# Routed rows turned by 64x64 products with an identity, eight tiles at a time, in rounds one and two of a convolution with routed experts

## The chip, the cores and the metric

The kernel runs on one core of a Trainium2 chip. The metric is the time of one execution on the device in microseconds (us); less is better. The change is judged by the median of several executions of each kernel.

## What is computed

The input `x` is 8 sequences of 5056 tokens with 128 channels; `h` is one filter of the same length for each channel. The first half is a causal convolution by way of a long Fourier transform, the second sends each of the 40,448 results to one of 16 experts, chosen in two steps.

```python
Xf = np.fft.rfft(x, n=L, axis=1); Hf = np.fft.rfft(h, n=L, axis=0)      # L = 2 * 5056
y = np.fft.irfft(Xf * Hf[None], n=L, axis=1)[:, :S]                     # then rows: x = y.reshape(N, 128)
g_idx = np.argmax(x @ w_group, axis=1)                                  # 4 groups, weight g_w by softmax
for g in range(4):
    xg = x[g_idx == g]; e_idx = np.argmax(xg @ w_expert[g], axis=1)     # 4 experts each, weight e_w by softmax
    for e in range(4):
        xe = xg[e_idx == e]
        out[rows of xe] = (g_w * e_w)[:, None] * (np.maximum(xe @ w1[g, e], 0) @ w2[g, e])
```

## The kernel before, in words

**Three rounds.** `ROUNDS` splits the filter and the 8 sequences into three rounds of three: the filter with sequences 0 and 1, then 2 to 4, then 5 to 7. For each round r, `stage1(r)` does the first part of the forward transform (lines 441 and 447, alternating: two of three steps by quadruples of 64x64 products, the third by 128x128 products), `groups(r)` does the rest of it, the multiplication by the filter and the first part of the inverse, pair of frequencies by pair (`forward` line 548, `multiply` line 568 on VectorE, `inverse` line 615, copied out of PSUM by ScalarE in line 631), and `side(r)` does the last part of the inverse and the routing. All of line 548's and line 615's products are 64x64 too, four of them in the four quarters of the array. Results between the parts go through HBM (`zd`, `zr`).

**The side work.** `side(r)` goes through 8 octaves of 8 of the 64 residues. For each octave it makes two lumps (`mm` line 756, `rest` line 771) that accumulate in the two PSUM banks `py0` and `py1`, and ScalarE copies them to `yT` (line 779): 128 channels on the partitions, T x 128 tokens along the row, T = 10 tiles in round one (r = 0) and 15 in the others. From `yT` come two things:

- the logits: `lm` multiplies `yT` by the routing weights in four column strips of 32 (line 829), ScalarE copies them to `lT` (line 835); `lt` turns `lT` by transposes (line 840), ScalarE copies them to `lg` (line 844), and `gate_math`, a row of small VectorE operations, finds expert, weight and place of each token;
- the rows to be sent: `rows(i)` turns four tiles of 128 tokens at a time by four 128x128 transposes into one bank (line 815), and one ScalarE copy (line 819) puts them into a tile `rw` in 16-bit halves. GpSimd then scatters each tile's 128 rows to the experts' lists in HBM (`scatter`, line 895).

`bank()` (line 798) hands out `py0` and `py1` in turn to `lm`, `lt` and `rows`; the lumps use the same two banks. Whoever writes a bank waits until ScalarE has copied what was there.

**What sets the order.** The program is written out in the order in which `weave` calls its pieces: a main list (stage 1 and groups, then the experts' matmuls) and beside each stretch of it one round's side work, whose pieces have due times (`at`, in eighths of a round). An engine executes its instructions in that order. The side work of round one lies beside round two's stage 1 and groups, that of round two beside round three's, that of round three beside the first experts' matmuls. Since the main list advances in steps of a stage 1 step, a forward pair or an inverse pair, two pieces with near due times can fall into the same gap and then stand directly one behind the other. The scatters are paced by a count of matmul time that the program keeps itself (`worked`, `clock`), not by a clock of the chip.

Names in the rows below: `pp` is a two-bank PSUM tile of stage 1 and groups, `cg` and `ns` the constants of a pair and their negative (made by ScalarE, line 526), `hg` the filter's spectrum, `zm` and `zt` what the lumps read back, `px`, `pz`, `ptr` PSUM tiles of the experts.

Of the kernel before, what the change touches and what calls it, by code (L numbers as in the profile page):

```python
# [13 lines left out]
U16 = mybir.dt.uint16  # L14
# [6 lines left out]
B, S, D = 8, 5056, 128  # L21
# [11 lines left out]
ROW = D + 2  # L33
# [10 lines left out]
COL, COLR = 4 / 2400, 1 / 2400 + 25e-6  # L44
NW_MAX = (NTOK + NE * 127) // BLK
T0, H0 = 1000, 2000
GP = 128
# [31 lines left out]
RH = 8  # L79
# [142 lines left out]
def columns(nu):  # L222

    n = 8 * nu * NH
    t = (n + GP - 1) // GP
    return t, n - (t - 1) * GP
# [11 lines left out]
class Kernel:  # L238
# [481 lines left out]
    def side(self, r):  # L720
        nc, cx = self.nc, self.cx
# [59 lines left out]
        def lump(k):  # L781
            def f():
                if k == 0 and r < 2:
                    nc.vector.memset(self.smask, 1.0)
                    first = self.smask[:, 0:NE * T].rearrange("p (e t) -> p e t", t=T)[:, :, 0:1]
                    nc.vector.memset(first, 0.0)
                for n in range(4 * k, 4 * k + 4):
                    mm(n)
                    if n % QB == QB - 1:
                        load(n // QB + 2)  # L790
                rest(4 * k)

            return f

        T, last = columns(nu)
        od = {}

        def bank():
            od["bank"] = 1 - od.get("bank", 1)
            return self.ps.tile([128, 512], F32, name=f"py{od['bank']}", bufs=1)  # L800

        def rows(i):

            if i == 0:
                od["rw"] = []
                od["o"] = od.get("o", -1) + 1
            if i % 2 == 0:
                while self.sends and self.sends[0][0] <= (8 * r + od["o"] - 2, i // 2):
                    self.send()
                od["rw"].append(cx.tile([128, RH, 2 * ROW], U16, name="rw", bufs=4))  # L810
            n = min(4, T - 4 * i)
            pt = bank()
            for j in range(n):
                k = (4 * i + j) * GP
                last = nc.tensor.transpose(  # L815
                    out=pt[:, j * D:(j + 1) * D], in_=self.yT[:, k:k + GP], identity=self.ident
                )
            self.worked(last, n * D * COL / 2)
            nc.scalar.copy(  # L819
                out=od["rw"][i // 2][:, 4 * i % RH:4 * i % RH + n, 0:2 * D].rearrange("p j (h d) -> p j h d", h=2),  # L820
                in_=pt[:, 0:n * D].bitcast(U16).rearrange("p (j d h) -> p j h d", d=D, h=2),
            )

        nsl = (T + 3) // 4

        def lm():
# [23 lines left out]
        def advance(g):  # L850
            return lambda: next(g, None)

        def both(*fs):
            return lambda: [f() for f in fs]

        at = []
        more = [lambda i=i: rows(i) for i in range(2, nsl)]
        for o in range(N2 // 8):
            math = {}
            ops = self.gate_math(od, math, b0 * S + o * 8, T, nu, REST if r < 2 else REST2)  # L860
            sends = [self.scatter(math, k, GP if k < T - 1 else last, r, T) for k in range(T)]
            if r < 2:
                t = 8 * o
                at.append((t, lump(2 * o), False))
                at.append((t + 3, lump(2 * o + 1), False))
                at.append((t + 4.7, both(lm, lambda: rows(0)), False))
                at.append((t + 6.4, both(lt, lambda: rows(1)), False))
                at.append((t + 9.5, both(*more), False))
                at += [(t + 6.5 + 5.6 * k / (NMATH + REST), advance(ops), True) for k in range(NMATH + REST)]
                at.append((t + 12.15, lambda o=o, s=sends: self.sends.extend(((8 * r + o, i // RH), f, self.clock + READY + SPREAD * i) for i, f in enumerate(s)), True))  # L870
            else:

                t = 6 * o
                at.append((t, lump(2 * o), False))
                at.append((t + 2, lump(2 * o + 1), False))
                at.append((t + 3, both(lm, lambda: rows(0)), False))
                at.append((t + 4, both(lt, lambda: rows(1)), False))
                at.append((t + 5, both(*more), False))
                at += [(t + 4.02 + 3.3 * k / (NMATH + REST2), advance(ops), True) for k in range(NMATH + REST2)]
                at.append((t + 7.4, lambda o=o, s=sends: self.sends.extend(((8 * r + o, i // RH), f, self.clock + READY + SPREAD * i) for i, f in enumerate(s)), True))  # L880
# [971 lines left out]
```

## Time and profile before

| what | value |
|---|---|
| runs | 1656.35, 1651.05, 1656.14 us, median 1656.14 |
| the profiled execution | 1647.12 us, span 1645.4 us |
| TensorE (PE) busy | 1586.1 us, 96% of the span |
| VectorE (DVE), ScalarE (ACT), GpSimd (POOL) busy | 80%, 66%, 46% |
| mean granted TensorE clock | 0.992 of full speed |
| side work of rounds one and two | from about 150 to 587 us of the span |
| line 815, all rounds | 320 transposes, 49.7 us busy |

A row of the timeline has the start in us from the span's start, the time from the first start to the last modelled end of the instructions merged in it, the engine (PE for matmuls, PEld for weight loads), the line, the operation, output and inputs by the program's names, shapes, and a count. A matmul's modelled end lies well after the moment at which the next one can start, so TensorE's pace is read from start to start, not from the second column. A matmul in float32 that isn't a transpose has two records in the trace, a transpose has one: "x32" of line 441 are 16 products.

### The profile page before, as it was taken

What the parts mean: (1) busy time and instruction counts of PE and PEld (TensorE: products, weight loads), DVE (VectorE), ACT (ScalarE), POOL (GpSimd) and SP (SyncE); (2) the same over time, 40 slices, a digit from 0 to 9 for tenths busy, and PEclk for the clock granted to TensorE, in tenths of its full rate; (3) what the DMA queues carried; (4) which work ended last, traced back from release to release, by engine and by line L of the source; (5) the groups of instructions that cost most, each with busy time, mean ns of one, the idle gap of its engine ahead of it and who ended that gap; (6) DMA issues with size and microseconds to landing.
All of it is one profiled execution on the core that took longest, in us unless ns stands there. A gap on an engine that the chain in (4) does not pass through costs nothing. (4 is left out here: it accounts for less than half of the span.)

```text
span 1645.4 us, 46854 instructions
## 1 busy us (share of the span) xinstructions
PE 1586.1 (96%) x16576; PEld 1241.5 (75%) x16576; DVE 1313.1 (80%) x2911; ACT 1092.4 (66%) x2161; POOL 760.0 (46%) x730
## 2 busy tenths in 40 slices
PE   8998999989999989999999999999999999999997
PEld 8776755557766547877777778788888888888997
DVE  6654699885688887788877788888888888887898
ACT  5564555545555556777777777677777777777875
POOL 1462144342465545155555556445555554334555
PEclk9999999999999989999999999999999999999999
DMA  7798688877789977766666655558866687555666
GB/s 209 237 294 240 185 259 268 277 226 223 216 273 302 289 209 190 191 172 177 181 169 179 176 142 151 146 139 235 196 155 171 163 233 181 138 137 151 172 171 166
DMA packets 400429, 328.58 MB, mean 200 GB/s; under 512 B 165740, under 2 KB 343921, under 8 KB 400168
## 3 DMA queue, kind: packets, MB, share of 16 engines
q1 hardware_dynamic: 371304, 269.43, 59.9%
q0 software_dynamic: 20608, 41.79, 7.5%
q10 hardware_dynamic: 8256, 14.10, 3.0%
q8 instruction: 137, 2.24, 0.6%
q14 instruction: 124, 1.02, 0.2%
HBM read 207.21 MB, written 96.08 MB: 184 GB/s over the span
## 5 line engine op out<-in xcount | busy, mean ns | idle before, releaser
L895 POOL DMA_INDIRECT srt<-rw,pos x320 | 336.6, 1052 | 390.7 <-PE py L815 61.7
L1512 POOL DMA_INDIRECT out<-orow,ids x188 | 195.8, 1041 | 222.5 <-PE px L1437 52.9
L1512 POOL DMA_INDIRECT out<-orow,sids x92 | 97.2, 1057 | 113.3 <-PE px L1441 46.3
L568 DVE TENSOR_TENSOR y<-pp,hg 128x768 f32<-128x768 f32 (+1 forms) x108 | 92.3, 855 | 60.2 <-ACT hg L558 31.6
L615 PE MATMUL pp<-y,cg 64*64 64x384 f32 (+1 forms) x1504 | 117.5, 443 | 6.6 <-DVE m L568 4.3
L548 PE MATMUL pp<-st,cg 64*64 64x192 f32 (+1 forms) x1588 | 117.4, 407 | 0.7 <-PE pp L615 0.4
L462 DVE TENSOR_TENSOR st<-pp,odd 128x320 f32<-128x320 f32 x96 | 46.9, 488 | 74.4 <-ACT odd L461 74.2
L631 ACT COPY zs<-pp 128x768 f32<-128x768 f32 (+1 forms) x106 | 75.7, 714 | 45.0 <-PE pp L615 35.3
L1446 DVE SCALAR_TENSOR_TENSOR h0l<-px,h0h 128x512 fp32r<-128x512 f32 (+1 forms) x109 | 73.3, 673 | 34.5 <-ACT h0h L1445 33.7
L1446 DVE SCALAR_TENSOR_TENSOR h2l<-px,h2h 128x512 fp32r<-128x512 f32 (+1 forms) x112 | 75.3, 672 | 29.7 <-ACT h2h L1445 27.8
L1445 ACT ACTIVATE h0h<-px 128x512 fp32r<-128x512 f32 (+1 forms) x109 | 63.9, 587 | 52.0 <-PE px L1441 48.0
L779 ACT COPY yT<-py 128x474 f32<-128x474 f32 (+1 forms) x96 | 44.2, 513 | 78.0 <-PE py L771 72.6
L1446 DVE SCALAR_TENSOR_TENSOR h3l<-px,h3h 128x512 fp32r<-128x512 f32 (+1 forms) x111 | 74.5, 671 | 26.1 <-ACT h3h L1445 25.2
L756 PEld LDWEIGHTS py<-ig,zm 126*64 126x64 f32 x2048 | 74.1, 137 | 26.8 <-ACT rw L819 9.8
L756 PE MATMUL py<-ig,zm 126*64 126x79 f32 x2048 | 82.8, 235 | 11.6 <-ACT rw L819 6.9
L548 PEld LDWEIGHTS pp<-st,cg 64*64 64x64 f32 x1588 | 60.8, 134 | 42.7 <-issue 35.4
L615 PEld LDWEIGHTS pp<-y,cg 64*64 64x64 f32 x1504 | 56.7, 133 | 47.0 <-issue 31.8
L568 DVE TENSOR_TENSOR m<-pp,hg 128x768 f32<-128x768 f32 (+1 forms) x108 | 91.5, 847 | 0.0
L599 POOL TENSOR_TENSOR y<-y,m 128x512 f32<-128x512 f32 x40 | 51.0, 1277 | 73.6 <-DVE m L589 40.9
L1445 ACT ACTIVATE h3h<-px 128x512 fp32r<-128x512 f32 (+1 forms) x111 | 65.3, 588 | 28.2 <-PE px L1441 27.3
L819 ACT COPY rw<-py 128x1024 uint16<-128x1024 uint16 (+1 forms) x88 | 80.8, 937 | 1.7 <-PE py L815 0.5
L1445 ACT ACTIVATE h1h<-px 128x512 fp32r<-128x512 f32 (+1 forms) x111 | 65.2, 587 | 21.7 <-PE px L1441 19.5
(479 smaller groups left out, 5087.7 us busy)
## 6 DMA issues: line engine op xcount, KB each, us to landing
wr<-in_moe_w SPq DMA_DIRECT2D x373, 256.0 KB
zm<-zd SPq DMA_DIRECT2D x64, 378.0 KB
cg<-in_c_g SPq DMA_DIRECT2D x106, 224.0 KB
zd<-zs SPq DMA_DIRECT2D x50, 384.0 KB
hg<-hd SPq DMA_DIRECT2D x68, 128.0 KB
xt<-in_x ACTq DMA_DIRECT2D x52, 160.0 KB
zm<-zd SPq DMA_DIRECT2D x32, 252.0 KB
zd<-zs SPq DMA_DIRECT2D x31, 256.0 KB
```

What stands on the lines that cost most here:

```text
L462: nc.vector.tensor_tensor(out=all_st[:, 0:2 * HALF, d], in0=even, in1=odd, op=ALU.add)
L548: last = nc.tensor.matmul(px[c * 64:c * 64 + 64, b, to], lhsT=k, rhs=data[:, of], start=begin, stop=i == len(steps) - 1 or p == 0 and i == ...
L568: nc.vector.tensor_tensor(out=t[:, :, 0:w].rearrange("p t (r u d) -> p t r u d", r=2, u=nu), in0=taken(px, part).unsqueeze(1).broadcast_to ...
L599: (nc.gpsimd if r == 0 else nc.vector).tensor_tensor(out=y[:, :, 0:w], in0=y[:, :, 0:w], in1=m[:, :, 0:w], op=ALU.add)
L615: last = nc.tensor.matmul(pz[c][h:h + 64, 0:w], lhsT=wt[c * 64:c * 64 + 64, k + h:k + h + 64], rhs=y[c * 64:c * 64 + 64, part, 0:w], start ...
L631: nc.scalar.copy(out=z[:, 0:n, 0:w], in_=pp[:, 0:n, 0:w])
L756: last = nc.tensor.matmul(pys[q][c:c + 64, col(n, u)], lhsT=zms[q][:, n % QB, k:k + 64], rhs=self.ig[:, 0:NH], start=n % QB == 0 and u == ...
L819: nc.scalar.copy(out=od["rw"][i // 2][:, 4 * i % RH:4 * i % RH + n, 0:2 * D].rearrange("p j (h d) -> p j h d", h=2), in_=pt[:, 0:n * D].bi ...
L895: ins = self.nc.gpsimd.indirect_dma_start(out=self.srt, out_offset=bass.IndirectOffsetOnAxis(ap=k["pos"][0:p, j:j + 1], axis=0), in_=k["rw ...
L1445: nc.scalar.activation(out=hh, in_=p, func=AF.Relu)
L1446: nc.vector.scalar_tensor_tensor(out=hl, in0=p, scalar=0.0, in1=hh.bitcast(F32), op0=ALU.max, op1=ALU.subtract)
L1512: ins = self.nc.gpsimd.indirect_dma_start(out=self.a["out"], out_offset=bass.IndirectOffsetOnAxis(ap=ids, axis=0), in_=o, in_offset=None, ...
```

## The change

In rounds one and two (r < 2) `rows` is no longer called. A new function `eight` turns up to eight tiles at a time, each by four plain products of a 64x64 block of `yT` with a 64x64 identity, in the four quarters of the array; the two halves of the channels go to two banks, and each bank is copied by one ScalarE copy for all eight tiles. `eight(0)` has a due time of its own, 5.6, between those of `lm` (4.7) and `lt` (6.4), which now stand alone; `eight(1)`, the remaining 2 tiles in round one and 7 in round two, takes the place of the last calls of `rows` at 9.5. Round three (r = 2) is as before.

```diff
--- before.py
+++ after.py
@@ -821,6 +821,32 @@
                 in_=pt[:, 0:n * D].bitcast(U16).rearrange("p (j d h) -> p j h d", d=D, h=2),
             )
 
+        def eight(i):
+
+            if i == 0:
+                od["rw"] = []
+                od["o"] = od.get("o", -1) + 1
+            while self.sends and self.sends[0][0] <= (8 * r + od["o"] - 2, i):
+                self.send()
+            t = cx.tile([128, RH, 2 * ROW], U16, name="rw", bufs=4)
+            od["rw"].append(t)
+            n = min(8, T - 8 * i)
+            pts = [bank(), bank()]
+            for j in range(n):
+                k = (8 * i + j) * GP
+                for b in (0, 64):
+                    for c in (0, 64):
+                        last = nc.tensor.matmul(
+                            pts[b // 64][c:c + 64, j * 64:j * 64 + 64], lhsT=self.yT[b:b + 64, k + c:k + c + 64],
+                            rhs=self.ident[b:b + 64, b:b + 64], start=True, stop=True, tile_position=(b, c),
+                        )
+            self.worked(last, n * D * COL / 2)
+            for b in range(2):
+                nc.scalar.copy(
+                    out=t[:, 0:n, 0:2 * D].rearrange("p j (h d) -> p j h d", h=2)[:, :, :, b * 64:b * 64 + 64],
+                    in_=pts[b][:, 0:n * 64].bitcast(U16).rearrange("p (j d h) -> p j h d", d=64, h=2),
+                )
+
         nsl = (T + 3) // 4
 
         def lm():
@@ -863,9 +889,10 @@
                 t = 8 * o
                 at.append((t, lump(2 * o), False))
                 at.append((t + 3, lump(2 * o + 1), False))
-                at.append((t + 4.7, both(lm, lambda: rows(0)), False))
-                at.append((t + 6.4, both(lt, lambda: rows(1)), False))
-                at.append((t + 9.5, both(*more), False))
+                at.append((t + 4.7, lm, False))
+                at.append((t + 5.6, lambda: eight(0), False))
+                at.append((t + 6.4, lt, False))
+                at.append((t + 9.5, lambda: eight(1), False))
                 at += [(t + 6.5 + 5.6 * k / (NMATH + REST), advance(ops), True) for k in range(NMATH + REST)]
                 at.append((t + 12.15, lambda o=o, s=sends: self.sends.extend(((8 * r + o, i // RH), f, self.clock + READY + SPREAD * i) for i, f in enumerate(s)), True))
             else:
```

In these two rounds 200 transposes become 800 products (8 octaves of 10 and of 15 tiles), and the 56 copies of line 819 become 64. The orders of VectorE, GpSimd and SyncE have the same instructions in the same places. Three places of TensorE's order follow; names with `py0` and `py1` are the two banks, `pp`, `cg`, `ns` and `y` belong to the groups, and what stands in brackets is what an instruction waits for.

TensorE before, round one's third octave: `lm`, `rows(0)`, a forward pair, `lt`, `rows(1)`.

```order
L829 MATMUL py0_3867<-yT_333,wge_113 32x384 [waits PE_49]
L829 MATMUL py0_3867<-yT_333,wge_113 32x384 x3
L815 MATMUL py1_3875<-ident_132,yT_333 128x128 [waits PE_49]
L815 MATMUL py1_3875<-ident_132,yT_333 128x128 x3
L548 MATMUL pp_3885<-st_94,cg_3436 64x384 x4
```

The same place in the changed kernel (line 855 is the old 829).

```order
L855 MATMUL py0_3931<-yT_333,wge_113 32x384 [waits PE_49]
L855 MATMUL py0_3931<-yT_333,wge_113 32x384 x3
L839 MATMUL py1_3939<-ident_132,yT_333 64x64 [waits PE_49]
L839 MATMUL py1_3939<-ident_132,yT_333 64x64
L839 MATMUL py0_3940<-ident_132,yT_333 64x64 [waits Activation_49]
L839 MATMUL py0_3940<-ident_132,yT_333 64x64
```

Here `eight(0)` stands directly behind `lm`, and its third product writes `py0`, into which `lm` has just written; the transposes before wrote the other bank.

TensorE before, round one's fifth octave: the end of a forward pair, `lt`, `rows(1)`, an inverse.

```order
L548 MATMUL pp_4802<-st_94,ns_4741 64x192 x3
L840 MATMUL py0_4828<-ident_132,lT_4764 128x128 [waits Activation_49]
L840 MATMUL py0_4828<-ident_132,lT_4764 128x128 x2
L815 MATMUL py1_4834<-ident_132,yT_333 128x128 [waits Activation_49]
L815 MATMUL py1_4834<-ident_132,yT_333 128x128 x3
```

The same place in the changed kernel (line 866 is the old 840); only the first and the last of the 32 products are shown.

```order
L548 MATMUL pp_4923<-st_94,ns_4869 64x192 x3
L839 MATMUL py1_4950<-ident_132,yT_333 64x64 x2
L839 MATMUL py0_4951<-ident_132,yT_333 64x64 [waits Activation_49]
...
L839 MATMUL py0_4951<-ident_132,yT_333 64x64 x2
L866 MATMUL py1_4986<-ident_132,lT_4892 128x128 [waits Activation_49]
L615 MATMUL pp_4992<-y_4822,xt_83 64x384 [waits DVE_49]
```

Here `lt` stands directly behind `eight(0)` and writes `py1`, the first of the two banks that `eight(0)` has filled.

## Rows read from the trace of the kernel before

**Rows 1.** The page: span, and busy time of TensorE.

```profile
span 1645.4 us, 46854 instructions
PE 1586.1 (96%) x16576; PEld 1241.5 (75%) x16576; DVE 1313.1 (80%) x2911; ACT 1092.4 (66%) x2161; POOL 760.0 (46%) x730
```

**Rows 2.** Busy time by stretch: stretch, its us, engines, clock, DMA.

```profile
200.00:390.00 190.00, 176.22 (x2936) 112.45 (x2936) 156.58 (x358) 94.75 (x225) 76.15 (x74) 0.98 0.81 252
...
437.00:600.00 163.00, 156.86 (x2490) 98.57 (x2483) 140.05 (x287) 87.52 (x196) 93.60 (x90) 0.99 0.88 272
```

**Rows 3.** Waits of ScalarE, 140 to 600 us: total, times, longest.

```profile
ACT ns L526 <- DMA cg<-in_c_g: 16.6, 5, 6.3
```

**Rows 4.** Timeline of TensorE: transposes, quarter products and changes between them.

```profile
169.24 0.60 PE L815 MATMUL py<-ident,yT 128*128 128x128 f32 x4
169.68 1.24 PE L447 MATMUL pp<-f,xy 128*128 128x158 f32 x8
170.85 0.78 PE L441 MATMUL pp<-f,xt 64*64 64x80 f32 x32
171.45 0.73 PE L441 MATMUL pp<-f,xy 64*64 64x80 f32 x32
172.11 1.31 PE L756 MATMUL py<-ig,zm 126*64 126x79 f32 x32
173.36 0.77 PE L771 MATMUL py<-igt,zt 64*64 64x158 f32 x16
174.06 1.34 PE L447 MATMUL pp<-f,xt 128*128 128x158 f32 x8
...
176.59 0.44 PE L815 MATMUL py<-ident,yT 128*128 128x128 f32 x2
176.87 1.24 PE L447 MATMUL pp<-f,xt 128*128 128x158 f32 x8
...
192.03 0.60 PE L815 MATMUL py<-ident,yT 128*128 128x128 f32 x4
192.56 0.51 PE L441 MATMUL pp<-f,xy 64*64 64x80 f32 x16
...
196.71 0.77 PE L771 MATMUL py<-igt,zt 64*64 64x158 f32 x16
197.29 0.46 PE L441 MATMUL pp<-f,xt 64*64 64x80 f32 x16
```

**Rows 5.** Timeline: the logits' copy beside the transposes behind `lm`.

```profile
164.87 0.89 PE L815 MATMUL py<-ident,yT 128*128 128x128 f32 x4
165.00 0.48 ACT L835 COPY lT<-py 128x384 f32<-128x384 f32 x1 [0.59 <-PE py L829]
```

**Rows 6.** Timeline, round one's seventh octave: the same copy, late.

```profile
317.95 0.66 PE L815 MATMUL py<-ident,yT 128*128 128x128 f32 x4
318.54 2.81 PE L615 MATMUL pp<-y,cg 64*64 64x384 f32 x32
322.43 0.31 ACT L526 ACTIVATE ns<-cg 128x128 f32<-128x128 f32 x1 [3.49 <-DMA cg<-in_c_g]
322.65 0.46 ACT L835 COPY lT<-py 128x384 f32<-128x384 f32 x1
323.16 0.55 PE L840 MATMUL py<-ident,lT 128*128 128x128 f32 x3 [1.81 <-ACT lT L835]
```

**Rows 7.** Timeline, round one's fifth octave: transposes, next work, their copy.

```profile
267.50 0.60 PE L815 MATMUL py<-ident,yT 128*128 128x128 f32 x4
268.04 2.17 PE L615 MATMUL pp<-y,xt 64*64 64x384 f32 x24
268.14 1.01 ACT L819 COPY rw<-py 128x1024 uint16<-128x1024 uint16 x1
```

**Rows 8.** Timeline, round two: seven transposes, next work, their copies, who waits.

```profile
452.85 0.98 PE L815 MATMUL py<-ident,yT 128*128 128x128 f32 x7
453.96 1.20 PE L548 MATMUL pp<-st,xt 64*64 64x384 f32 x16
456.83 1.72 ACT L819 COPY rw<-py 128x1024 uint16<-128x1024 uint16 x2
457.89 1.31 PE L756 MATMUL py<-ig,zm 126*64 126x79 f32 x32 [1.11 <-ACT rw L819]
```

## The prediction

> **What bounds the kernel now.** I read the page first, then the busy time by stretch, then who waits for whom, and last the timeline of TensorE. On the page TensorE is busy for 96% of the span, far ahead of the other engines [rows 1]: what shortens its stream shortens the kernel, as long as TensorE does not wait for something else. The change lies in the groups of rounds two and three and the stage 1 before each; TensorE is busy there for 176.2 of 190 us and for 156.9 of 163 [rows 2], so about 6% of this time is already spent waiting, partly because ScalarE, which executes in order, stands for a constant's load (16.6 us in five waits) and so keeps TensorE from its banks [rows 3]. I therefore count time in TensorE's stream at 94% of its worth, and a wait for ScalarE in full.
>
> In the timeline the reader is to see two things. First, the pace: four transposes pass in 0.44 us from start to start, 0.11 each [rows 4]. Second, the price of a change between 128-wide work (lines 447, 815, 840) and quarters of the array (lines 441, 771, 548, 615), which shows where the same group stands before different neighbours [rows 4]: four transposes take 0.44 us before line 447 and 0.53 before line 441, so leaving 128-wide work for quarters costs 0.09. Sixteen records of line 771 take 0.58 before line 441 and 0.70 before line 447, so leaving quarters for 128-wide work costs 0.12. Two transposes behind quarters take 0.28 where 0.22 would do, so entering costs 0.06, and I take the same 0.06 for entering quarters. A pair of changes costs 0.33 us, one change 0.165.
>
> **The change part by part.**
>
> *Fewer changes of shape: a gain.* Counted over TensorE's whole order, 46 of 368 changes go: in most octaves `rows(0)` stood between `lm` and the groups' quarters and the last `rows` stood alone among quarters, and now both are quarters themselves. 46 x 0.165 = 7.6 us; at 94%, 7.1 us. The places with 32-column strips (`lm`) I price like the others, since no row shows `lm` before quarters. Bounds: a change costs at least the smallest leaving, 0.09, and at most the largest leaving with an entry, 0.18; that makes 3.9 and 7.8 us. I stay near the upper end, since every one of these changes has both parts.
>
> *The products themselves: nothing.* 200 transposes of 0.11 us go, 200 quadruples of products with 64 columns come. No row shows 64 columns. The 64 records of line 441, eight quadruples of 80 columns, take 1.26 us with one entry and one exit [rows 4]; less 0.16 for these, 0.1375 for one quadruple. If time goes with the columns, 64 of them take 0.110, as much as a transpose. If short products pass no faster than those of 80 columns, it is 0.1375, and 200 x 0.0275 = 5.5 us are lost. The nearest rows to decide are those of line 771: with almost twice the columns its quadruples take about twice as long (0.58 less 0.06, by two, 0.26 us for 158 columns), so columns set the pace, and I take zero and keep 5.5 for the range.
>
> *`eight` needs both banks: a loss behind `lm`.* In three octaves (the third and seventh of round one, the fourth of round two) `eight(0)` stands directly behind `lm`. The third product writes the bank that ScalarE is still to copy to `lT`. In the trace this copy ends 0.61 us after the point at which the work behind `lm` starts (164.87 to 165.48) [rows 5]; until now the transposes filled this time. 3 x 0.61 = 1.8 us. It can be more where ScalarE is late: in the seventh octave the copy ended 5.2 us after that point, since ScalarE waited for a load; before, an inverse pair of 2.7 us lay in this time and TensorE idled for 1.81 [rows 6]. That the inverse now comes behind the wait would cost 2.7 us there instead of 0.6.
>
> *`lt` behind `eight(0)`: a loss.* In three others (round one's fifth, round two's third and eighth) `lt` stands directly behind `eight(0)` and writes the bank that ScalarE copies first. In the trace the copy of such a bank starts 0.10 us after TensorE can go on and takes 1.01 [rows 7]: 1.11 us each, 3.3 together. Before, `lt` found a free bank. What is queued behind it on TensorE is an inverse or forward pair, so all of it is late; VectorE's logits arithmetic waits with it, but has about a fifth of its time free [rows 2].
>
> *What costs nothing.* In the other ten octaves a pair of 1.7 us or more lies between `eight(0)` and `lt`, and covers the first copy of 1.01. ScalarE gets 8 more copies, each cheaper than the 1.01 of a four-tile one, and is busy for about half of these stretches [rows 2]; if that cover went, as where ScalarE is late, the second copy's 1.01 would fall on whoever waits next (first rival). The scatters on GpSimd, the loads on SyncE and VectorE's operations stand in the same places; the kernel's own count of matmul time gets the same sum, one entry for eight tiles.
>
> Sum: -7.1 + 1.8 + 3.3 + 0 = -2.0 us. The profiled execution, 1647.1, would become 1645.1. It lies 9 us below the median of the three runs, 1656.1, so for a median I take **1654.1 us**. About 0.3%, 5 us, is what a measurement of this kernel can tell from no change: the forecast is no change that can be told.
>
> One rule speaks against the change. The Trainium skill (Perfetto Trace Analysis, section Transposes) asks that logical transposes be made as transposes and not as matmuls, since these skip the arithmetic; it gives no price. By it the sum would be 5.5 us worse if the upper bound above is what it means; the rows of line 771 speak for the lower, so I keep it in the range alone.
>
> **The rivals.**
>
> *ScalarE is late in most octaves (slower).* Two copies of 1.01 now stand in one piece behind `eight(0)`, where before one stood behind `lm` and one behind `lt`. In round two the same burst exists already: seven transposes end at 453.96, their two copies start only at 456.83, 2.9 us later, behind other work of ScalarE, and the lump that needs the bank idles for 1.11 [rows 8]. If ScalarE is on average half as late behind `eight(0)`, 1.45 us, the first copy ends 2.5 us after it; the cover is 1.7 to 2.7, and with the waits passed on to the next pair I count 0.8 in each of the ten octaves. That is 8 us more: 1662 us. It decides from a lag of 0.7 us on, the 1.7 of cover less 1.01. Against it: most of the time ScalarE is idle in these stretches.
>
> *Issue sets the pace of short products (slower).* The 64 records of line 441 pass at 0.0197 us each, changes included [rows 4]. If that is what TensorE can issue, a tile of 8 records takes 0.158 whatever its columns, 0.048 more than a transpose: 200 x 0.048 = 9.6 us, 1663.7 us. Against it stands that line 771 is slower by its columns, for it that nothing shorter is in the trace. The Trainium skill (TensorE: Matmul & The Clock Gate, section "Wait — 56ns, not 53.3ns?") states a floor of about 25 ns from start to start however short a matmul is; taken for each record it would make 0.2 us of a tile and 1672 us of the kernel. The trace does not agree: 64 records in 1.26 us are under 20 ns each.
>
> *The waits lie where TensorE waits anyway (faster).* About 20 us of waits stand in the two stretches [rows 2]. If the six places only shift these, the 7.1 us stay whole: 1649.0 us. For it: in the seventh octave TensorE stood still in any case [rows 6]. Against it: the other five show no such wait.
>
> *Loads set the time (no change).* If late loads, not TensorE, decide when the next pair can start, the gain and the six waits both end in front of them, and the time stays 1656.1 us. For it: single waits for a load reach 6.3 us [rows 3]. Against it: TensorE is busy for 93 to 96% of the two stretches [rows 2].
>
> **How the numbers follow.** Forecast 0.50; ScalarE late 0.10; issue 0.08; waits absorbed 0.24; loads 0.08. Faster by over 0.3% (below 1651.2) is the third rival with 0.05 from the forecast's edge: 0.29. Slower (above 1661.1) is the first two with 0.03 from the edge: 0.21. The rest, 0.50, is no change. The range goes from 1648, just below the third rival's 1649.0, to 1663, which takes in the upper bound for the products (1659.6) and the first rival and leaves out most of the issue case.
>
> **What would show it.** Right: line 839 in bursts of 32 products (64 records) that take about 0.88 us between quarters; no gap at the change from and to lines 548 and 615; line 839 waiting for `lT` some 0.6 us in three octaves and line 866 waiting for `rw` 1.1 us in three others. Wrong: bursts of 1.1 us or more (price of products), waits for `rw` at line 866 in most octaves (first rival), or none of these waits at all (third). A time outside 1648 to 1663 would mean that something moved which no term here has, such as the loads or the scatters.

## The result: slower by 0.7%

| | before | changed |
|---|---|---|
| median of 8 runs each | 1655.26 us | 1664.08 us |
| lowest and highest | 1651.05 to 1659.12 | 1659.62 to 1669.64 |
| the profiled execution | 1647.12 us | 1668.74 us |

The ratio is 1.0068, 95% interval 1.0049 to 1.0087: slower, by 8.8 us between the medians and by 11 by this ratio, which is not that of the medians (1.0053). The forecast was 1654.1 us, range 1648 to 1663: wrong in its sign and just outside its range. The two profiled executions lie 21.6 us apart, over twice as far as the medians; the changed one is some 5 us behind at the first lump already, before any changed instruction. So single profiles are compared here place by place, and times by medians.

The page of the changed kernel has about the same busy time of TensorE as [rows 1] in a longer span.

```profile
span 1666.9 us, 49642 instructions
PE 1588.2 (95%) x17976; PEld 1260.3 (76%) x17976; DVE 1314.8 (79%) x2911; ACT 1090.3 (65%) x2169; POOL 760.8 (46%) x730
```

The two stretches of [rows 2] in the changed kernel (same columns): TensorE is busy 2 to 3 us less in each, though the work in them is not quite the same, since the changed execution is 11 to 20 us behind there.

```profile
200.00:390.00 190.00, 173.48 (x3295) 114.93 (x3297) 157.62 (x358) 93.84 (x235) 75.40 (x73) 0.97 0.76 239
437.00:600.00 163.00, 154.77 (x3280) 107.91 (x3284) 133.47 (x292) 87.79 (x197) 91.49 (x87) 0.98 0.83 260
```

What it waits for, 140 to 640 us of the changed kernel (total us, times, longest; line 839 is the products, 845 their copies, 855, 861, 866 and 870 are the old 829, 835, 840 and 844):

```profile
PE pp L441 <- issue: 6.9, 6, 3.7
PE py L839 <- ACT lT L861: 5.9, 4, 3.9
PE py L756 <- ACT rw L845: 4.5, 3, 2.9
PE py L866 <- ACT rw L845: 4.0, 4, 1.4
...
PE pp L441 <- ACT lg L870: 1.1, 2, 0.6
PE pp L441 <- ACT rw L845: 0.9, 1, 0.9
```

The same view of the kernel before has, of the side work's own waits:

```profile
PE py L756 <- ACT rw L819: 6.9, 4, 3.2
PE py L840 <- ACT lT L835: 1.8, 1, 1.8
PE pp L441 <- ACT rw L819: 0.6, 1, 0.6
PE py L815 <- ACT rw L819: 0.4, 1, 0.4
```

The reader is to see two new lines, 5.9 and 4.0 us, where one of 1.8 goes. They come from the six places of the forecast and two more, of 1.26 and 0.27 us. The lumps' own wait for these copies (line 756) falls from 6.9 to 4.5. In the timeline of the changed kernel, `lt` behind `eight(0)` (round one's fifth octave):

```profile
277.24 1.17 PE L839 MATMUL py<-ident,yT 64*64 64x64 f32 x64
277.88 0.31 ACT L560 ACTIVATE hg<-hg 128x128 f32<-128x128 f32 x1 [2.45 <-DMA hg<-hd]
278.10 0.29 ACT L526 ACTIVATE ns<-cg 128x128 f32<-128x128 f32 x1
278.69 1.93 ACT L845 COPY rw<-py 128x1024 uint16<-128x1024 uint16 x2 [0.29 <-PE py L839]
...
279.75 0.55 PE L866 MATMUL py<-ident,lT 128*128 128x128 f32 x3 [1.34 <-ACT rw L845]
```

And `eight(0)` behind `lm` in the seventh octave, the place of [rows 6]:

```profile
329.38 0.85 PE L855 MATMUL py<-yT,wge 128*32 128x384 f32 x8
330.16 0.33 PE L839 MATMUL py<-ident,yT 64*64 64x64 f32 x4
333.62 0.31 ACT L526 ACTIVATE ns<-cg 128x128 f32<-128x128 f32 x1 [4.27 <-DMA cg<-in_c_g]
333.84 0.46 ACT L861 COPY lT<-py 128x384 f32<-128x384 f32 x1
...
334.35 1.15 PE L839 MATMUL py<-ident,yT 64*64 64x64 f32 x58 [3.86 <-ACT lT L861]
```

ScalarE stands for the load of a constant, so the copy to `lT` that frees the bank is late. Before, the inverse pair of 2.7 us lay in that time and only `lt` waited, 1.81 us; now TensorE idles through it, 3.86 us.

The larger of the two places that the forecast had not named is round one's second octave, where the same copy is late with only stage 1 between `lm` and the burst:

```profile
196.79 0.48 ACT L861 COPY lT<-py 128x384 f32<-128x384 f32 x1 [1.28 <-DMA zm<-zd]
197.33 0.33 PE L839 MATMUL py<-ident,yT 64*64 64x64 f32 x5 [1.26 <-ACT lT L861]
```

An undisturbed burst passes at the forecast pace, with nothing lost at its edges:

```profile
248.28 0.51 PE L548 MATMUL pp<-st,ns 64*64 64x192 f32 x8
248.60 1.11 PE L839 MATMUL py<-ident,yT 64*64 64x64 f32 x64
249.53 0.83 PE L615 MATMUL pp<-y,cg 64*64 64x384 f32 x8
```

From start to start 0.93 us for eight tiles, 0.116 a tile.

### The profile page after: what moved, and what is told of

It is laid out like the page before. It is cut to its first block, busy times and chain, and to the rows that moved or that the text cites. A ratio compares the mean times of both kernels' runs of the same rounds, so it can differ in the third digit from the quotient of the medians.

```text
span 1666.9 us, 49642 instructions
## 1 busy us (share of the span) xinstructions
PE 1588.2 (95%) x17976; PEld 1260.3 (76%) x17976; DVE 1314.8 (79%) x2911; ACT 1090.3 (65%) x2169; POOL 760.8 (46%) x730
## 3 DMA queue, kind: packets, MB, share of 16 engines
q14 instruction: 125, 1.02, 0.2%
## 5 line engine op out<-in xcount | busy, mean ns | idle before, releaser
L615 PEld LDWEIGHTS pp<-y,cg 64*64 64x64 f32 x1504 | 62.2, 134 | 45.3 <-issue 26.1
L756 PE MATMUL py<-ig,zm 126*64 126x79 f32 x2048 | 85.1, 240 | 10.7 <-DMA zm<-zd 6.0
L1472 ACT ACTIVATE h2h<-px 128x512 fp32r<-128x512 f32 (+1 forms) x112 | 65.8, 587 | 19.7 <-PE px L1468 13.9
```

The source lines that it names most:

```text
L615: last = nc.tensor.matmul(pz[c][h:h + 64, 0:w], lhsT=wt[c * 64:c * 64 + 64, k + h:k + h + 64], rhs=y[c * 64:c * 64 + 64, part, 0:w], start ...
L756: last = nc.tensor.matmul(pys[q][c:c + 64, col(n, u)], lhsT=zms[q][:, n % QB, k:k + 64], rhs=self.ig[:, 0:NH], start=n % QB == 0 and u == ...
L1472: nc.scalar.activation(out=hh, in_=p, func=AF.Relu)
```

## The experiments

Fourteen runs were made in four jobs, each job on another chip; some repeat a kernel. Ratios are against the kernel before on the same chip, whose median was 1670.7, 1654.5, 1649.6 and 1674.4 us in the four.

**First job.** Three theories: T1, waits for a bank where `eight(0)` touches `lm` or `lt`; T2, two ScalarE copies in one piece; T3, the products cost more than the transposes.

*e1_last*: products for the rest of an octave alone.

```diff
-                at.append((t + 4.7, lm, False))
-                at.append((t + 5.6, lambda: eight(0), False))
-                at.append((t + 6.4, lt, False))
+                at.append((t + 4.7, both(lm, lambda: rows(0)), False))
+                at.append((t + 6.4, both(lt, lambda: rows(1)), False))
```

> Only the last tiles of an octave (2 in round one, 7 in round two) are turned by products; the first eight are turned by transposes next to lm and lt, as before the change. The change as a whole cost 0.68%, about 11 us. Theory one, bank waits where eight(0) stands next to lm or lt (3 places each): none of them is left here, two changes of shape per octave are saved (16 x 0.33 = 5 us), so 0.1 to 0.4% faster than before. Theory two, the two ScalarE copies in one piece behind eight(0) delay what follows in every octave: round two's last tiles had two copies in one piece before as well, so the same 0.1 to 0.4% faster. Theory three, the products themselves cost more than the transposes: 88 of the 200 tiles are products here, so about 44% of the loss stays, 0.3% slower.

*e2_first*: the opposite, `eight(0)` by products, the rest by transposes.

```diff
-                at.append((t + 9.5, lambda: eight(1), False))
+                at.append((t + 9.5, both(*more), False))
```

> Only the first eight tiles of an octave are turned by products, at the place of eight(0); the last ones are turned by transposes as before the change. Theories one (bank waits) and two (copies in one piece) put the whole loss into eight(0): 0.7 to 1.0% slower than before. Theory three (price of the products): 112... 128 of 200 tiles, about 0.4% slower.

*e3_place*: the change's places, all rows by transposes.

```diff
-                at.append((t + 5.6, lambda: eight(0), False))
+                at.append((t + 5.6, both(lambda: rows(0), lambda: rows(1)), False))
-                at.append((t + 9.5, lambda: eight(1), False))
+                at.append((t + 9.5, both(*more), False))
```

> All tiles are turned by 128x128 transposes into banks of four, as before the change, but the first eight stand together at the place of eight(0), with lm and lt alone; so the order and the two copies in one piece are those of the change, the products are not. Where they stand next to lm, the bank that lm wrote is needed only by the fifth tile, and the first bank is full, and can be copied, four tiles earlier. Theory one (bank waits): about two thirds of the waits stay, 0.3 to 0.5% slower than before, plus the lost gain of fewer changes of shape. Theory two (copies in one piece): 0.6 to 0.8% slower, like the change. Theory three (price of the products): no slower than before by more than 0.2%.

*e4_apart*: the change with other due times in six octaves, so that of the six octaves in which the pieces touch one is left (round two's third, where `eight(0)` then stands behind `lm`).

```diff
-                at.append((t + 4.7, lm, False))
-                at.append((t + 5.6, lambda: eight(0), False))
+                lms = {(0, 2): 4.0, (0, 4): 4.0, (0, 6): 4.0, (1, 2): 4.0, (1, 3): 4.0, (1, 7): 4.0}
+                at.append((t + lms.get((r, o), 4.7), lm, False))
+                first = {(0, 2): 5.2, (0, 4): 5.2, (1, 2): 5.2, (1, 7): 5.2}
+                at.append((t + first.get((r, o), 5.6), lambda: eight(0), False))
```

(`lump(2 * o + 1)` of round one's third octave moves from 3 to 2.0.)

> The change as it is, but in six octaves lm, eight(0) and one lump get other due times, so that a forward or inverse pair lies between lm and eight(0) and between eight(0) and lt; of the six places where they touched, one is left (behind lm, round two's third octave). Theory one (bank waits): the loss goes, between 0.2% faster and 0.2% slower than before. Theory two (copies in one piece): 0.5 to 0.7% slower, as the change. Theory three (price of the products): 0.6 to 0.7% slower, as the change.

Measured: e1_last 1.0046 (1.0027 to 1.0065), e2_first 1.0155 (1.0128 to 1.0181), e3_place 1.0059 (1.0040 to 1.0077), e4_apart 1.0082 (1.0055 to 1.0110). No theory fits all four: e1_last, which T1 and T2 had faster, is slower, as T3 has it; e4_apart speaks against T1; and e3_place is 0.59% slower without a single product, where T3 allowed 0.2. And the profiles show something that no theory had: on this chip bursts of products break off in the middle, while TensorE waits for nothing that the profile shows. The timeline of e1_last, a burst of 28 products that should take 0.81 us and takes over 3:

```profile
502.15 0.51 PE L839 MATMUL py<-ident,yT 64*64 64x64 f32 x17
...
502.98 0.36 PE L839 MATMUL py<-ident,yT 64*64 64x64 f32 x3 [0.32 <-issue]
...
503.73 0.36 PE L839 MATMUL py<-ident,yT 64*64 64x64 f32 x4 [0.39 <-issue]
...
504.47 0.55 PE L839 MATMUL py<-ident,yT 64*64 64x64 f32 x19 [0.39 <-issue]
```

The waits of TensorE sum it up, 140 to 640 us of e4_apart (total, times, longest):

```profile
PE py L839 <- issue: 8.3, 21, 1.3
```

And 400 to 640 us of e1_last:

```profile
PE py L839 <- issue: 5.3, 16, 0.4
```

The changed kernel's first profile has one such break, 0.4 us. So this job mixes two losses.

**Second job.** Theory A: the order costs (`lm` and `lt` alone, two copies in one piece). Theory B: TensorE's instructions arrive too slowly for short products. *e5_before* and *e6_after* are the two kernels unchanged.

> The kernel before, unchanged, for its profile beside the others of this job. Theory A (the order costs: lm and lt stand alone and two copies of ScalarE follow one another behind the first eight tiles): as many breaks without a wait on TensorE up to the first exchange product as in e3_place, about 38 with 19 us, and fewer microseconds of waits for ScalarE in front of the py banks than the 16 us of the change's profile. Theory B (TensorE's instructions arrive too slowly when short products need two instructions every 7 ns): fewer breaks than e1_last and e4_apart had (53 and 45), and none inside the transposes of the routed rows. Its time is the reference: ratio 1.000.

> The change, unchanged, on the chip of this job. Both theories: ratio 1.005 to 1.009. Theory B: if this chip is one on which bursts of products break off (as in e1_last, e2_first and e4_apart: 13 to 21 breaks of 0.35 to 1.5 us), the ratio is 1.008 or more, and the breaks are there; if the profile shows none, as on the chip of the first result, 1.007 or less. Theory A: the ratio has nothing to do with breaks, and the profile has about 6 us of waits for lT and 10 us for rw in front of the py banks.

*e7_half*: the same turn with half the instructions, two products of 64 rows to 128 columns for a tile.

```diff
-                    for c in (0, 64):
-                        last = nc.tensor.matmul(
-                            pts[b // 64][c:c + 64, j * 64:j * 64 + 64], lhsT=self.yT[b:b + 64, k + c:k + c + 64],
-                            rhs=self.ident[b:b + 64, b:b + 64], start=True, stop=True, tile_position=(b, c),
-                        )
+                    last = nc.tensor.matmul(
+                        pts[b // 64][:, j * 64:j * 64 + 64], lhsT=self.yT[b:b + 64, k:k + GP],
+                        rhs=self.ident[b:b + 64, b:b + 64], start=True, stop=True, tile_position=(b, 0),
+                    )
```

> The change with two products of 64 rows to 128 columns for each tile in place of four to 64: the same 64 columns of data, half the weight loads and products, the same places, banks and copies. Theory B: no bursts that break off, and 3 to 8 us less than e6_after, ratio about 1.003 to 1.005. Theory A: as e6_after within 2 us. A third one, C (the shape of the array is what the change saves on): the pieces change the shape again against the 64x64 work around them, 32 pieces with two changes of 0.165 us, so 10 us more than e6_after at most, ratio up to 1.013, if changes cost what was forecast and nothing else moves.

*e8_fours*: e3_place with the first eight tiles in two pieces of four.

```diff
-                at.append((t + 5.6, both(lambda: rows(0), lambda: rows(1)), False))
+                at.append((t + 5.2, lambda: rows(0), False))
+                at.append((t + 5.9, lambda: rows(1), False))
```

> All routed rows by transposes, and every piece alone: lm at 4.7, the first four tiles at 5.2, the second four at 5.9, lt at 6.4, the rest at 9.5. Against e3_place only the first eight tiles are split into two pieces of four. Theory A in the form that two copies of ScalarE in one piece cost: back to the kernel before, 0.999 to 1.002. Theory A in the form that lm and lt without rows behind them cost (their product waits for a bank or their copy is not covered): as e3_place, 1.004 to 1.008. Theory B: nothing here has more instructions than before, so 1.000, plus up to 36 more changes of shape of 0.165 us (6 us, 1.004) where a piece of four now stands between other work.

Measured: e5_before 1.0013 (0.9992 to 1.0033), e6_after 1.0075 (1.0053 to 1.0097), e7_half 1.0184 (1.0161 to 1.0208), e8_fours 1.0022 (1.0000 to 1.0044). On this chip bursts hardly break off (twice in e6_after, 1.5 us together, never in e7_half), and still the change loses as much as in the first result: B does not explain it. Half the instructions made it 19 us slower than e6_after (timeline of e7_half):

```profile
249.50 2.00 PE L838 MATMUL py<-ident,yT 64*128 64x64 f32 x32
251.43 0.88 PE L615 MATMUL pp<-y,cg 64*64 64x384 f32 x8
```

1.93 us for eight tiles where the change takes 0.93. Merged rows don't show why, but the single starts do. In the change four records start within 20 ns, the next four 58 ns after the first, and a weight load starts 2 or 3 ns behind each product, ahead of the product that it is for. In e7_half two records start 7 ns apart, taken to be one of each half, and the next two 112 ns after them; their weight loads start 56 ns behind the products before them and some 50 ahead of their own, so the starts of loads and products take turns. The Trainium skill (TensorEngine Tiling (Array Packing), Key Properties) says that different tiles can load weights and multiply in parallel. The trace agrees for the four quarters; for the two halves it shows products in pairs, but no load that starts beside a product.

With two undisturbed profiles of each kernel the **price of a piece** can be taken, from the start of the last product before it to the start of the first behind it, less that last product's own pace. The usual values, in us, worked out from single starts, round one and round two:

| piece of an octave | before | changed |
|---|---|---|
| `lm` (before: with `rows(0)`) | 1.48, 1.69 | 0.89, 1.11 |
| `eight(0)` | | 0.93, 0.93 |
| `lt` (before: with `rows(1)`) | 1.02, 1.13 | 0.59, 0.70 |
| the rest, 2 or 7 tiles | 0.48, 1.02 | 0.23, 0.81 |
| sum of an octave | 2.98, 3.84 | 2.64, 3.55 |

Undisturbed, the change saves 8 x (0.34 + 0.29) = 5.0 us; 4.7 with each octave's own value. With their waits the pieces of rounds one and two take 57.2 and 58.9 us in the two profiles of before, 62.9 and 61.9 in those of the change: the waits turn a gain into a loss of about 4.

**Third job.** Theory D: a piece is worth its price, and the first job's losses were its breaks. Theory E: products slow a later stage. *e9_last* is e1_last again, *e12_apart* is e4_apart, *e13_after* the change.

> The kernel of e1_last once more (first eight tiles by transposes beside lm and lt as before, only the rest of an octave by products). By the price of each piece on TensorE, taken from its last neighbour before to its first behind in the profiles of before and of the change, a rest of two tiles falls from 0.48 to 0.23 us and one of seven from 1.02 to 0.81 us: 8 x 0.25 + 8 x 0.21 = 3.7 us. Theory D (the pieces are worth their price, and e1_last lost because bursts of products broke off on that chip without a wait, 10 us): ratio 0.997 to 0.999 if the profile shows fewer than five such breaks, 1.003 to 1.006 if it shows fifteen or more as e1_last did. Theory E (products make a later stage slower, whatever the bursts do): 1.003 to 1.006 in either case.

> The kernel of e4_apart once more (the change with other due times in six octaves, so that one place is left where the eight tiles touch lm or lt). By the pieces the change saves 54.2 - 49.5 = 4.7 us undisturbed and loses 12 to 13 us in waits, 10 of them at the six places where the pieces touch. Theory D: without breaks in the bursts 0.998 to 1.001, the waits of L839 for lT and of L866 for rw under 2 us together; with fifteen breaks or more as in e4_apart 1.006 to 1.009. Theory A in its form (two copies of ScalarE in one piece cost wherever they stand): 1.005 to 1.008 without breaks too.

> The change, unchanged, on the chip of e9_last and e12_apart. Theory D: 1.006 to 1.009 without breaks, with the six waits at the same places (third and seventh octave of round one and fourth of round two in front of L839, fifth of round one, third and eighth of round two in front of L866), 9 to 11 us together; over 1.010 if bursts break off. Theories A and E: 1.005 to 1.009 in either case.

Measured: e9_last 0.9981 (0.9965 to 0.9997), e12_apart 1.0036 (1.0020 to 1.0051), e13_after 1.0094 (1.0066 to 1.0122). The bursts stay nearly whole: none breaks in e9_last, one by 0.5 us in e12_apart, one by 0.2 in e13_after. The rest of an octave by products gains 3.0 us, where its prices say 3.7; E falls. In the timeline of e9_last a rest of two tiles stands between neighbours of their own shape, in that of e5_before it stands between two changes:

```profile
282.56 0.82 PE L615 MATMUL pp<-y,cg 64*64 64x384 f32 x8
283.21 0.41 PE L839 MATMUL py<-ident,yT 64*64 64x64 f32 x16
283.44 1.15 PE L548 MATMUL pp<-st,cg 64*64 64x384 f32 x16
```

The same place in e5_before, two transposes:

```profile
282.23 0.44 PE L815 MATMUL py<-ident,yT 128*128 128x128 f32 x2
282.60 1.20 PE L548 MATMUL pp<-st,cg 64*64 64x384 f32 x16
```

0.23 against 0.37 us from start to start, and 0.11 more at the entry, which merged rows don't show.

Taking five of the six places away gives back 1663.17 - 1655.59 = 7.6 us, and the waits say where. In e13_after, 140 to 640 us:

```profile
PE py L839 <- ACT lT L861: 5.7, 4, 4.6
PE py L866 <- ACT rw L845: 5.1, 5, 1.8
```

In e12_apart:

```profile
PE py L866 <- ACT rw L845: 1.9, 2, 1.6
PE py L839 <- ACT lT L861: 1.0, 2, 0.6
```

10.8 us become 2.9. That is T1, which the first job seemed to refute: the waits account for some 8 of the 13.6 us that the change loses on this chip. But 6 us of loss stay, more than D allowed (1.001).

**Fourth job.** Theory F: those 6 us come from the order. Theory G: from the products. *e14_rows* is e12_apart by transposes alone.

```diff
-                at.append((t + first.get((r, o), 5.6), lambda: eight(0), False))
-                at.append((t + 9.5, lambda: eight(1), False))
+                at.append((t + first.get((r, o), 5.6), both(lambda: rows(0), lambda: rows(1)), False))
+                at.append((t + 9.5, both(*more), False))
```

> The places of e12_apart, but every routed row by transposes again: rows(0) and rows(1) together at the place of the eight tiles, the rest at 9.5. Theory F (what e12_apart still loses, 6 us, comes from the order: eight tiles in one piece, whose two copies of 0.9 us keep ScalarE 1.8 us from what it would do next): as slow as e12_apart plus what the products save there, about 4 us, 1.004 to 1.007. Theory G (what is left comes from the products and their two banks): 0.999 to 1.002.

*e15_vector*: e12_apart with one of the two copies behind `eight(0)` on VectorE.

```diff
-                nc.scalar.copy(
+                (nc.vector.tensor_copy if i == 0 and b == 1 else nc.scalar.copy)(
```

> e12_apart with the second of the two copies behind the first eight tiles on VectorE in place of ScalarE, 16 copies in all; same products, banks and places. Theory F: ScalarE is free 0.9 us earlier 16 times, so e12_apart's 1.0036 falls towards 1.000, unless VectorE, which is 80% busy in this stage, gives it back: then its waits of the group m at L568 grow above the 12 us that e12_apart shows. Theory G: 1.003 to 1.006.

*e16_last* is e1_last a third time.

> The kernel of e1_last and e9_last a third time, to see whether it holds against the kernel before. Theory D: 0.997 to 0.999 if the bursts stay whole; 1.003 to 1.006 if they break off fifteen times or more. The rest of an octave by products is worth 3.7 us by its pieces, 0.998.

Measured: e14_rows 1.0020 (0.9998 to 1.0041), e15_vector 1.0098 (1.0064 to 1.0133), e16_last 1.0031 (1.0011 to 1.0051). On this chip bursts break off as in the first job: 23 times with 9.0 us in e15_vector, and in e16_last, from 400 us on:

```profile
PE py L839 <- issue: 5.1, 15, 0.5
```

e14_rows, the only one of the three without such bursts, is the only one whose interval reaches no change. Its 1.0020 is at the edge of G's range (1.002) and under F's (1.004), but the interval reaches 1.0041, and e12_apart did not run on this chip; so F and G can't be told apart. The copy on VectorE brought nothing that shows beside the breaks: 1.0098 where e4_apart, on the other chip with breaks, had 1.0082. The third kernel repeats the first: e1_last and e16_last lose 0.46 and 0.31% where bursts break, e9_last gains 0.19% where they don't.

## Why the prediction was wrong

| step | predicted, us | shown, us |
|---|---|---|
| fewer changes of shape, and the products | -7.1 + 0 | -4.7 |
| `eight(0)` behind `lm` | +1.8 | +5.9 (3.8 and 5.7 in e6_after and e13_after), one place more than forecast |
| `lt` behind `eight(0)` | +3.3 | +4.0 (4.1 and 5.1) |
| the old wait of `lt` for `lT`, gone | inside the second line | -1.8 (2.8 in e5_before) |
| outside these pieces | 0 | +4 to +9, cause open |

*The gain was right in kind and too large.* Of the 7.1 us 4.7 came. 200 tiles at 0.116 in place of 0.110 us take 1.2 of the difference; the rest is the price of a change, about 0.13 where a piece shows it alone (a rest of two tiles by transposes takes 0.48, 0.22 for its tiles and 0.13 for each of two changes) against 0.165 forecast. That the products cost nothing held within this 1.2; the bound of 5.5 and the rival that issue sets the pace at 0.158 a tile are out, on undisturbed bursts. The rule of the Trainium skill (Perfetto Trace Analysis, Transposes) is thus worth 1.2 us here, less than the changes of shape that breaking it saves.

*The step that failed is the price of the wait behind `lm`.* All six places were named, and the two short ones behind `lm` came out somewhat under the 0.61 forecast: third octave 0.34 us idle, 0.67 from the start of the burst to its third product; round two's fourth 0.44 idle. The seventh octave was priced at 0.61 in the sum although [rows 6] showed the copy 5.2 us late; "2.7 us there instead of 0.6" stood beside the sum as something that could happen. It was the case that the one trace in hand showed, and it came: 3.86 us here, 4.61 in e13_after, less the 1.81 that `lt` waited there before. A fourth place was missed: in round one's second octave the quarters of stage 1 between `lm` and the burst don't cover the copy, which was late by a load (1.26 us idle). In the terms of the rivals this is "ScalarE is late", at these places and not in the other octaves, where line 866 waits once, 0.27 us.

*The second step that failed is the zero for everything else:* "what costs nothing" cost about as much as the mispriced wait. The medians differ by 8.8, 10.6 and 13.6 us in the three comparisons on chips where bursts stay whole, the pieces with their waits by 5.0 in the mean of the profiles (e13_after, with 64.4, taken in). The prediction had said what a time outside its range would mean, that something moved which no term has, and so it is. In the third job e9_last keeps the old order and gains nearly its prices; e12_apart, with the change's order and fewer waits, has pieces that sum to 56.3 us, less than before, and is yet 6 us slower. e8_fours (0.22%) and e14_rows (0.20%) change the order too and lose some 3 us by these ratios without products, though the medians of e8_fours differ by only 1.0. That the other order costs something beyond the waits of its own pieces fits all three, but the intervals of two of them reach no change, and the cause was not found.

Two things on record narrow it. The granted clock is a small part: its mean over the runs, as a share of full speed, was 0.9882 in e6_after against 0.9893 before, 0.9888 in e13_after against 0.9908, an estimated 2 and 3 us at these times of 1650 to 1665; in e12_apart, 0.9914, it was no lower than before, and the 6 us stay. And part of the rest may lie in stage 1 of round three, whose own products the change leaves alone. From the last product of round two's groups to the first of round three's, side work included, the profiles have 79.4 and 85.4 us before, 81.9 in e9_last and 80.1 in e8_fours, but 85.2, 85.9 and 85.1 in the change and 85.8 in e12_apart. Two profiles of one kernel lie 6 us apart there, so this is a place to look and not a cause.

No version beats both kernels everywhere. The best is e9_last, 0.19% faster than before on a chip where bursts stay whole, and the same kernel is 0.3 to 0.5% slower on two where they don't.

## What to carry to other kernels

When a piece is given two buffers instead of one, list what stands directly before and behind it in the order of its engine: it now waits for both neighbours' evacuations, and one such place held TensorE for 3.9 us, 2.0 more than before, as much as fifteen saved changes of array shape. If a trace shows a copy late once, price the new wait at that lateness, not at the undisturbed one. And look whether a loss comes from the same place on a second chip before a theory is dropped for it.

## What the runs showed of the hardware that was not expected

- Whether dense bursts of short products stay whole differed from chip to chip: on two of the four, bursts of 56 to 64 records, most of them after 430 us, broke off up to three times in every kernel that had them, mostly with 0.2 to 0.5 us of idle time each, 13 to 23 breaks in a profile; on the others at most twice. The kernel before is 16 to 25 us slower on those two chips as well. The instruction pages that the DMA queues brought took much the same mean time in both, 1.12 to 1.20 us for each of some 140, so that does not explain it; the cause is open.
- Two products of 64 rows by 128 columns in the two halves took 0.224 us a tile, with weight loads and products in turn; four of 64 by 64, with loads beside products, took 0.116. Half the instructions were no help.
